# One order of instructions against another: half matmul groups, two token tiles' statistics on ScalarE, row maxima on GpSimd

## The chip, the core and the metric

The kernel runs on one core of a Trainium2 chip. The core has five engines that run their own instruction streams in order and meet only at semaphores: TensorE (PE, matmuls), VectorE (DVE), ScalarE (ACT), GpSimd (POOL) and SyncE (SP, here used only to issue DMAs). The metric is the device time of one execution in microseconds, the median of several runs. The kernel before takes 1212.65 us (three runs, 1212.34 to 1212.93).

## The reference

The input x is 2048 tokens by 512 features, in bf16. It is layer-normalised without scale or shift, and the result feeds two branches whose outputs are added to x:

```python
xn = _layernorm(x, axis=-1)
return x + _A_ref(xn, A_wqkv, A_wo) + _B_ref(xn, B_w1, B_w3, B_w2)

# A: 32 heads of 16 channels, every token attends to every token
scores = einsum("bhqd,bhkd->bhqk", q, k) * (16 ** -0.5)
o = softmax(scores) @ v            # then @ wo
# B: 512 -> 1792 -> 512
h = silu(xn @ w1) * (xn @ w3)      # then @ w2
```

The attention has 32 x 2048 x 2048 scores. Each must be part of a row maximum, and each must go through an exponential; nothing else in the computation has that many elements.

## The kernel before, in words

Four heads are a group: their 16-channel keys and queries lie in the four 32-partition strips of `KT` and `QT`, so four small matmuls run beside each other in TensorE. There are 8 groups of heads and 4 chunks of 512 queries, so 32 pairs of a chunk and a group. A pair is cut into *units* of 256 queries, the first pair into 128, 128 and 256, and the last three pairs into units of 128 (`units`, line 286).

The scores of a unit are computed twice.

- **Pass 1** (`p1_cand`, line 853). 128 queries of two heads against 512 keys, two matmuls into two PSUM banks (line 878). There are two such pairs of banks, 0-1 and 2-3. VectorE reduces each pair by one instruction, 1024 elements per partition to two maxima (line 900), into `part`. There are 1024 of these steps. The kernel calls them by their number n.
- **Final maximum** (`final_max`, line 906). Once all reductions of a unit are done, one more VectorE reduction takes the maximum over the four key chunks and negates it (line 941). GpSimd splits it into two bf16 parts in `Z` (lines 917 and 919). A transposing DMA and two row DMAs (lines 938 and 934) put these into rows 16 and 17 of each strip of `QT`, where the keys have ones, so that the next matmul subtracts the maximum by itself. For the first two units and the last four (`FAST_AUG`) a TensorE tile and a ScalarE copy do it instead (`tile_QT2`, line 684).
- **Pass 2** (`p2_cand`, line 974). The scores again, transposed, 128 keys by the unit's queries, one bank of 512 columns at a time (line 1014), in banks 4 to 7. ScalarE applies the exponential to a bank (line 1027), 2048 times in all, into one of 34 slots of `PT` (16 of them hold x at the start).
- **PV** (`tile_PV`, line 1035). Probabilities times V, with a column of ones in V that gives the denominator. ScalarE copies the result out (line 1091). The denominators go through DMAs and GpSimd (lines 1112 to 1136) to the normalised output. For the last three units VectorE does it with a reciprocal (line 1081).

Beside this run the *side tiles*, which accumulate in one bank and are then copied out by ScalarE: the transposes of the normalised input (`tile_tr`), the projections of K, Q and V, the gated network (`ffn_pair`: tiles G and U, three ScalarE instructions, lines 735 to 741, and three on GpSimd, lines 720 to 724), and the output tiles (`tile_OUT`). The results of the gated network wait in a ring of `NHT` = 28 slots of `hT`. The last four output tiles are made in two parts: `tile_OUTA` holds x and the gated network, `tile_OUTB` (VectorE, line 831) adds the eight head groups once they are normalised. A side tile is a list of *groups*, each of four matmuls of 512 columns in the four column strips (`col_groups`, line 487).

The order of all instructions is computed on the host before the program is emitted. `_Prog` keeps a clock for each engine from the constants at its top (`_VIS`, `_c_act`, `_c_dve`, `_c_mm`), and a loop takes again and again the step that could start first. `pick_pe` chooses between pass 1, pass 2 and a side group. A side group is taken if it ends before the moment when VectorE or ScalarE would run out of work (`late`). If none is ready and too little was issued lately (`low_load`), a *fill* is taken: four matmuls of the identity into a free bank, whose result nobody reads (`fill_cand`). What is decided by these clocks is then a fixed order. At run time each engine follows it and waits where it must.

The start: four DMAs bring x, four token tiles each (line 428). VectorE takes statistics of 16 token tiles (lines 502 and 505), GpSimd turns them into a factor (lines 515 to 523), VectorE normalises 12 tiles (line 530) and ScalarE four (line 535). Transposes, keys of group 0 and queries of group 0 follow, and then pass 1 can begin.

Of the kernel before, what the change touches and what calls it, by code (L numbers as in the profile page):

```python
# [13 lines left out]
_VIS = {"act": 0.155, "dve": 0.143, "pool": 0.085}  # L14
# [6 lines left out]
class _Item:  # L21
    __slots__ = ("fn", "reads", "writes", "occ", "lat", "cb", "pred", "name")

    def __init__(self, fn, reads, writes, occ, lat=None, cb=None, pred=None, name=""):
        self.fn = fn
        self.reads = reads
        self.writes = writes
        self.occ = occ
        self.lat = lat
        self.cb = cb  # L30
        self.pred = pred
        self.name = name


class _Prog:
# [3 lines left out]
    def __init__(self):  # L39
# [8 lines left out]
        self.pe_vis = 0.0  # L48

# [54 lines left out]
    def op(self, eng, fn, reads=(), writes=(), occ=0.1, lat=None, name="", first=None):  # L104
# [9 lines left out]
        op.vis = start + (occ + _VIS.get(eng, 0.1) if lat is None else lat)  # L114
        return self._add(op, reads, writes)

    def pe_start(self, mode, groups, ready):
        t = max(self.free["pe"], ready)
        if mode == "col":
            t = max(t, max(self.rg) + (0.09 if self.pe_mode == "row" else 0.0))  # L120
        else:
            t = max(t, max(self.rg[g] for g in groups))
            if self.pe_mode == "col":
                t = max(t, max(self.rg) + 0.104)
        return t

    def pe(self, fn, reads, writes, mode, groups, dur, name="", first=None):
# [8 lines left out]
        start = self.pe_start(mode, groups, ready)  # L136
        for g in (range(4) if mode == "col" else groups):
# [6 lines left out]
        if mode == "row":  # L144
            op.vis = max(self.pe_vis + 0.043, start + dur + 0.203)
# [60 lines left out]
class _Tile:  # L206
    __slots__ = ("groups", "evac", "name", "bank", "pred", "need", "on_start", "paced")

    def __init__(self, name, groups, evac, pred=None, need=None, on_start=None, paced=False):
        self.name = name  # L210
        self.paced = paced
        self.groups = groups
# [7 lines left out]
def _c_act(n):  # L220
    return n / 1200.0 + 0.063


def _c_dve(n):
    return n / 960.0 + 0.066


def _c_mm(n):
    return n / 2400.0 + 0.003
# [6 lines left out]
def _build(nc, A_x, A_wqkv, A_wo, B_w1, B_w3, B_w2, out):  # L236
# [16 lines left out]
    PV_LEFT = 4  # L253
    ROW_LEAD = 0.55
# [4 lines left out]
    NHT = 28  # L259
    UNIT_HEAD = (128, 128, 256)  # L260
    UNIT_TAIL = {1: (128, 128, 128, 128), 2: (128, 128, 128, 128), 3: (128, 128, 128, 128)}
    NFAST = 4
    NFPV = 3
# [12 lines left out]
    LOAD_WIN = 2.3  # L276
    LOAD_MIN = 14500
# [10 lines left out]
    NU = len(units)  # L288
    FAST_AUG = {0, 1} | set(range(NU - NFAST, NU))
# [8 lines left out]
    with ctx:  # L298
# [18 lines left out]
        wq_last = sb("wq_last", [128, DC * 4, 32], BF16)  # L317
# [15 lines left out]
        part = sb("part", [128, 2, 2, 4, NQC], FP32)  # L333
        negm = sb("negm", [128, 2, 8], FP32)
# [19 lines left out]
        OP_KEYS = [[("t1",)], [("a32",)], [("th", 0), ("th", 1)], [("zg", 0), ("zg", 1)]]  # L354

# [35 lines left out]
        poolq = {k: [] for k in ("z", "ln", "nrm", "ffn", "pad")}  # L391
# [1129 lines left out]
```

## Time and profile before

| what | value |
|---|---|
| median of three runs | 1212.65 us |
| profiled execution, first to last instruction | 1210.1 us |
| VectorE busy | 1191.3 us, 98% |
| ScalarE busy | 1160.9 us, 96% |
| TensorE busy (ends modelled) | 1158.3 us, 96% |
| GpSimd busy | 360.9 us, 30% |
| first pass-1 reduction starts | 18.47 us |
| last final maximum starts | 1190.91 us |

The profile page and the answers of the trace give the profiled execution. No time of its own is listed for it beside its span, so the 2.55 us between the span and the median stand for what lies around the instructions. Times are in microseconds from the first instruction unless ns is written. A busy time is the union of the records of an engine. Records of successive instructions on one engine overlap a little: a pass-1 reduction has a record of 1.21 us, but the next starts 1.13 us after it. So rates are read from starts, not from the mean of one record.

### The profile page before, as it was taken

To read this page: it belongs to the slowest core of one execution; us is meant where nothing else is said; L and a number is where in the kernel's file an instruction comes from. 1 tells how busy PE (TensorE), PEld (TensorE's weight loads), DVE (VectorE), ACT (ScalarE), POOL (GpSimd) and SP (SyncE) were. 2 spreads that over 40 slices of the span, in tenths; PEclk is the share of its full clock that TensorE was granted. 3 is DMA by queue.
4 is the path that set the end of the run, shared out by engine and by line. 5 is a ranking of instruction groups with operands and counts; after the bars stand their busy time and mean duration, and the time that the engine had idled before them with its cause. 6 is when DMAs were issued, how large, how long until landed. Compare 5 with 4: busy or idle time off the path is not lost.

```text
span 1210.1 us, 40652 instructions
## 1 busy us (share of the span) xinstructions
PE 1158.3 (96%) x17633; PEld 460.6 (38%) x17633; DVE 1191.3 (98%) x1154; ACT 1160.9 (96%) x2382; POOL 360.9 (30%) x470
## 2 busy tenths in 40 slices
PE   5999999999999999999999999999999999999998
PEld 2433333333333333333333333333333333334554
DVE  8999999999999999999999999999999999999995
ACT  5789999999999999999999999999999999999997
POOL 2234443635421135453111115553111111112210
PEclk9999999999999999999999999999999999999999
DMA  5422323222101022211001112211000111000000
GB/s 165 124 59 64 79 54 89 53 61 55 40 24 29 27 59 47 51 42 29 22 20 29 31 37 59 57 37 25 22 16 19 37 28 30 21 25 19 17 13 23
DMA packets 130303, 52.61 MB, mean 43 GB/s; under 512 B 99396, under 2 KB 130124, under 8 KB 130124
## 3 DMA queue, kind: packets, MB, share of 16 engines
q1 hardware_dynamic: 130124, 50.01, 16.4%
q8 instruction: 138, 2.26, 0.8%
q14 instruction: 41, 0.34, 0.1%
HBM read 38.73 MB, written 6.74 MB: 38 GB/s over the span
## 4 chain that ended last, share of the span: by engine, by line
ACT 49%; PE 33%; DVE 13%; issue 2%; POOL 1%; DMA 1%; SPq 0%; POOLq 0%
ACT PT L1027 42%; PE ps L491 18%; DVE part L900 13%; PE ps L1014 9%; PE ps L878 5%; ACT th L735 2%; ACT zg L737 2%; ACT U L1091 1%; ACT ub L741 1%; ACT kq L642 1%; PE ps L599 1%; ACT xnT L564 1%; DMA wk_on<-in_A_wqkv_dram 0%; POOL Rc L1116 0%; POOL hT L724 0%
## 5 line engine op out<-in xcount | busy, mean ns | idle before, releaser
L900 DVE TENSOR_REDUCE part<-ps 128x2 f32<-128x1024 f32 x1024 | 1167.8, 1214 | 1.8 <-PE ps L878 0.7
L1027 ACT ACTIVATE PT<-ps 128x512 bf16<-128x512 f32 x2048 | 1045.7, 650 | 6.1 <-PE ps L1014 5.0
L1014 PE MATMUL ps<-QT,KT 32*128 32x256 bf16 (+1 forms) x4544 | 566.9, 262 | 4.2 <-DVE wk_on L1083 0.3
L878 PE MATMUL ps<-KT,QT 32*128 32x512 bf16 x2048 | 437.6, 383 | 2.9 <-DVE part L900 2.3
L1014 PEld LDWEIGHTS ps<-QT,KT 32*128 32x128 bf16 x4544 | 215.7, 92 | 265.7 <-issue 108.0
L1116 POOL TENSOR_TENSOR Rc<-Lc,mone 128x8 f32<-128x8 f32 (+1 forms) x68 | 104.3, 1534 | 384.7 <-DMA Lc<-U 384.5
L491 PE MATMUL ps<-PT,Vaug 128*17 128x256 bf16 (+1 forms) x4544 | 191.0, 264 | 4.6 <-ACT zg L737 2.1
L491 PE MATMUL ps<-xnT,ident 128*32 128x512 bf16 x2048 | 162.0, 384 | 7.4 <-DVE part L900 0.5
L491 PE MATMUL ps<-xnT,w 128*32 128x512 bf16 x1792 | 149.0, 385 | 13.1 <-ACT zg L737 7.0
L878 PEld LDWEIGHTS ps<-KT,QT 32*128 32x128 bf16 x2048 | 113.6, 91 | 123.9 <-DVE part L900 56.4
L491 PEld LDWEIGHTS ps<-PT,Vaug 128*17 128x17 bf16 x4544 | 85.9, 89 | 100.6 <-issue 76.5
L722 POOL TENSOR_TENSOR a<-zg,ub 128x512 f32<-128x512 bf16 x56 | 64.6, 1153 | 61.8 <-ACT ub L741 61.6
L491 PE MATMUL ps<-w,hT 128*32 128x512 bf16 x896 | 79.7, 386 | 0.0
L724 POOL TENSOR_TENSOR hT<-a,t 128x512 bf16<-128x512 f32 x56 | 71.1, 1270 | 3.1
L491 PEld LDWEIGHTS ps<-xnT,w 128*32 128x32 bf16 x1792 | 39.3, 94 | 81.8 <-issue 72.1
L491 PEld LDWEIGHTS ps<-xnT,ident 128*32 128x32 bf16 x2048 | 40.1, 94 | 68.7 <-ACT PT L1027 50.1
L917 POOL TENSOR_SCALAR Z<-negm 128x8 bf16<-128x8 f32 (+1 forms) x70 | 15.7, 225 | 168.3 <-DVE negm L941 167.8
L1136 POOL TENSOR_TENSOR wk_on<-U,R 128x256 bf16<-128x256 f32 (+1 forms) x35 | 23.0, 658 | 105.2 <-DMA R<-rd 105.2
L1136 POOL TENSOR_TENSOR on_b<-U,R 128x256 bf16<-128x256 f32 (+1 forms) x33 | 23.4, 711 | 81.6 <-DMA R<-rd 81.5
L737 ACT ACTIVATE zg<-ps 128x512 bf16<-128x512 f32 x56 | 36.0, 643 | 0.0
L720 POOL TENSOR_SCALAR t<-th 128x512 f32<-128x512 bf16 x56 | 34.6, 618 | 4.6 <-ACT th L735 2.5
L741 ACT ACTIVATE ub<-ps 128x512 bf16<-128x512 f32 x56 | 35.7, 637 | 0.0
(78 smaller groups left out, 377.6 us busy)
## 6 DMA issues: line engine op xcount, KB each, us to landing
w<-in_B_w_dram SPq DMA_DIRECT2D x112, 128.0 KB
R<-rd SPq DMA_DIRECT2D x57, 128.0 KB
QT<-qd SPq DMA_DIRECT2D x31, 128.0 KB
KT<-kd SPq DMA_DIRECT2D x28, 128.0 KB
PT<-in_A_x_dram SPq DMA_DIRECT2D x4, 512.0 KB
xr<-in_A_x_dram SPq DMA_DIRECT2D x16, 128.0 KB
out_dram<-osb SPq DMA_DIRECT2D x16, 128.0 KB
qd<-kq SPq DMA_DIRECT2D x15, 128.0 KB
```

The lines of the kernel that those rows point to most:

```text
L491: ins = e.matmul(bank(bk)[32 * i:32 * i + m, c0:c0 + ncols], make_lhsT(i), rhs_ap(i), start=start, stop=stop, tile_position=(0, 32 * i), **kw)
L720: q.append(_Item(lambda e: e.tensor_scalar(t1[:, :], th[:, ss, :], 1.0, 1.0, ALU.mult, ALU.add), [("th", ss)], [("t1",)], 0.62, 0.72))
L722: q.append(_Item(lambda e: e.tensor_tensor(a32[:, :], zg[:, ss, :], ub[:, ss, :], ALU.mult), [("zg", ss), ("ub", ss)], [("a32",)], 1.1, 1.25))
L724: q.append(_Item(lambda e: e.tensor_tensor(hT[:, hslot(idx), :], a32[:, :], t1[:, :], ALU.mult), [("a32",), ("t1",)], [("hT", hslot(idx))] ...
L737: _Item(lambda e: e.activation(zg[:, ss, :], bank(bk), ACTF.Identity, scale=0.5), [("ps", bk)], [("zg", ss)], _c_act(512), cb=part_done, n ...
L741: return [_Item(lambda e: e.activation(ub[:, ss, :], bank(bk), ACTF.Identity), [("ps", bk)], [("ub", ss)], _c_act(512), cb=part_done)]
L878: ins = e.matmul(bank(2 * sl + i), QT[32 * j:32 * j + 32, qs, q * 128:(q + 1) * 128], KT[32 * j:32 * j + 32, g, kc * 512:(kc + 1) * 512], ...
L900: redq.append(_Item(lambda e: e.tensor_reduce(part[:, par, qt, 2 * pair:2 * pair + 2, kc], ps[:, sl * 1024:(sl + 1) * 1024].rearrange("p ( ...
L1014: ins = e.matmul(bank(b)[:, i * nq:(i + 1) * nq], KT[32 * j:32 * j + 32, g, (k0 + i) * 128:(k0 + i + 1) * 128], QT[32 * j:32 * j + 32, qs, ...
L1027: expq.append(_Item(lambda e: e.activation(PT[:, sl, :], bank(b), ACTF.Exp, scale=SCALE), [("ps", b)], [("PT", sl)], _c_act(512), cb=cb))
L1116: poolq["nrm"].append(_Item(lambda e: e.tensor_tensor(Rc[:, pp, 0:nl], Lc[:, pp, 0:nl], mone[:, 0:nl], ALU.pow), [("Lc", pp), ("mone",)], ...
L1136: poolq["nrm"].append(_Item(lambda e: e.tensor_tensor(onorm[ob][:, g, q0:q0 + nq], U[:, us, 0:nq], R[:, pp, 0:nq], ALU.mult), [("U", us)] ...
```

## The change

- *Half groups.* `col_groups` can issue a 512-column group as two of 256 columns. `pick_pe` takes a half where a whole group would end too late, and a half where little was issued lately.
- *Constants of the order.* New costs for ScalarE, VectorE and TensorE, among them a cold TensorE for the first 8 us; new leads and thresholds; another rule for fills, by a level that drains at 5000 columns per us and a window of 2.9 us; fills of ones at the very start.
- *The start.* x comes as 2, 2, 4, 4 and 4 tiles; the first 64 columns of the weights of K and Q come as small tiles of their own (`wk0c`, `wq0c`), ahead of the rest. Statistics of token tiles 2 and 3 are taken by ScalarE, by two activations with an accumulated sum. Eight tiles are normalised by VectorE and eight by GpSimd. Pass 1 of the first three units may go in the order in which key chunks get ready. V tiles may start earlier.
- *Final maxima.* For all units outside `FAST_AUG` the maximum over four key chunks is computed by six GpSimd instructions. Those of the first two units and the last four stay on VectorE.
- *The end.* The last four pairs, not three, go in units of 128. `tile_OUTA` takes six of the eight head groups, `tile_OUTB` the other two. The augmentation tiles (now `AQ`) get a bank before other tiles.
- *Memory.* `NHT` is 24, not 28.
- *Without effect.* `SPLIT` is empty, `PAIR_DEPTH` is 1, `MATE` is 0 and `TILE_BANKS` is None, so split rows, joined exponentials and bank choices in the new code never happen.

```diff
-    PV_LEFT = 4
-    ROW_LEAD = 0.55
+    PV_LEFT = 6
+    ROW_LEAD = 0.45
+    PAIR_DEPTH = 1
-    NHT = 28
+    NHT = 24
+    NGA = 6
-    UNIT_TAIL = {1: (128, 128, 128, 128), 2: (128, 128, 128, 128), 3: (128, 128, 128, 128)}
+    UNIT_TAIL = {i: (128,) * 4 for i in range(1, 5)}
-    LOAD_WIN = 2.3
-    LOAD_MIN = 14500
+    LOAD_RATE = 5000.0
+    LOAD_CAP = 3000.0
+    LOAD_MIN = 3000.0
+    RECENT = 2.9
+    RECENT_MIN = 9400.0
+    SPLIT = {u: ((1, 3),) for u in range(NU, NU)}
...
+        load_x(0, 2)
+        load_x(2, 4)
+        load_x(4, 8)
+        load_w(wk0c[:, :, :], [("wk0c",)], 1, 64)
+        load_w(wq0c[:, :, :], [("wq0c",)], 0, 64)
+        load_x(8, 12)
+        load_x(12, 16)
+        load_w(wv, WV_KEYS, 2)
+        load_w(wk, [("wk",)], 1)
+        load_w(wq[:, :, :], [("wq",)], 0)
...
+            f = part(0, ncols, start, skip or ncols == 512)
+            if ncols == 512:
+                f.halves = part(0, 256, start, True), part(256, 512, False, True)
             return f
...
+        LN_GROUPS = ((0, 2), (2, 4), (4, 8), (8, 12), (12, 16))
+        NORM = "ddpdp"
+        STATS = "dadddd"
...
+            if on_act:
+                for t in tl:
+                    miscq.append(_Item(lambda e, t=t: e.activation(
+                        a32[:, :], x_sb[:, t, :], ACTF.Identity, scale=1.0 / D, accum_out=mv[:, t, 0:1]),
+                        [("PT", t)], [("a32",), ("mv", t)], 0.57, 0.7))
+                for t in tl:
+                    miscq.append(_Item(lambda e, t=t: e.activation(
+                        a32[:, :], x_sb[:, t, :], ACTF.Square, scale=-1.0, bias=mv[:, t, 0:1],
+                        accum_out=mv[:, t, 1:2]),
...
+                p4 = part[:, par, 0:nqt, :, :].rearrange("p a j k -> p (a j) k")
+                d2, m2 = mx[:, 0, 0:4 * nqt, :], mx[:, 1, 0:4 * nqt, :]
+                poolq["z"] += [
+                    _Item(lambda e: e.tensor_tensor(d2, p4[:, :, 0:2], p4[:, :, 2:4], ALU.subtract), keys, [M0], 0.27),
+                    _Item(lambda e: e.tensor_scalar(d2, d2, BIG, 0.0, ALU.min, ALU.max), [M0], [M0], 0.27),
+                    _Item(lambda e: e.tensor_tensor(m2, d2, p4[:, :, 2:4], ALU.add), keys + [M0], [M1], 0.27),
+                    _Item(lambda e: e.tensor_tensor(d2[:, :, 0], m2[:, :, 1], m2[:, :, 0], ALU.subtract),
+                          [M1], [M0], 0.27),
+                    _Item(lambda e: e.tensor_scalar(d2[:, :, 0], d2[:, :, 0], 0.0, -BIG, ALU.min, ALU.max),
+                          [M0], [M0], 0.27),
+                    _Item(lambda e: e.tensor_tensor(ng, d2[:, :, 0], m2[:, :, 1], ALU.subtract),
+                          [M0, M1], [("negm", par)], 0.27)]
+                z_items()
...
+            if u not in FAST_AUG:
+                pool_max()
+                return None
...
-            groups = [g_on(qc, ts, g, g == 0, g == NG - 1) for g in range(NG)]
+            groups = [g_on(qc, ts, g, g == NGA, g == NG - 1) for g in range(NGA, NG)]
...
             if c[0] + c[2] <= late + TOL:
                 return c[0], c[1]
+            if recent_cols(c[0]) < RECENT_MIN and c[0] <= end + URG_WAIT:
+                return c[0], c[3] if len(c) > 3 else c[1]
+            if len(c) > 3:
+                if c[0] + _c_mm(256) <= late + TOL:
+                    return c[0], c[3]
             return go(x)
```

532 lines of the change are left out of this document (411 added, 121 removed).

## The prediction

> **What bounds the kernel now.** I read the busy shares first, then the chain that ended last, then busy time by stages, and last the reductions one by one. The first two seem to disagree:
>
> ```profile
> span 1210.1 us, 40652 instructions
> PE 1158.3 (96%) x17633; PEld 460.6 (38%) x17633; DVE 1191.3 (98%) x1154; ACT 1160.9 (96%) x2382; POOL 360.9 (30%) x470
> ...
> ACT 49%; PE 33%; DVE 13%; issue 2%; POOL 1%; DMA 1%; SPq 0%; POOLq 0%
> ```
>
> VectorE is the busiest, but the chain runs mostly over ScalarE. The stages (start:end and length, then busy us and instructions of PE, PEld, DVE, ACT, POOL, granted clock, DMA) decide it:
>
> ```profile
> 400.00:450.00 50.00, 49.16 (x698) 18.62 (x694) 50.00 (x48) 46.79 (x97) 13.42 (x18) 1.00 0.16 41
> ...
> 850.00:900.00 50.00, 48.25 (x714) 17.69 (x709) 49.91 (x48) 49.91 (x104) 8.22 (x11) 1.00 0.08 21
> ...
> 950.00:1000.00 50.00, 49.81 (x676) 18.39 (x668) 50.00 (x48) 46.33 (x95) 8.39 (x12) 1.00 0.11 30
> ```
>
> VectorE is full in each. ScalarE is full in one and idles 3 to 4 us in the others, where it has caught up and waits for rows whose maxima aren't there. So VectorE sets the pace, with ScalarE close behind: in windows of 25 us from 75 to 1200 us ScalarE idles about 20 us. Now VectorE's own stream (start, length of the run, count):
>
> ```profile
> 132.29 0.17 DVE L941 TENSOR_REDUCE negm<-part 128x8 f32<-128x32 f32 x1
> 132.38 18.19 DVE L900 TENSOR_REDUCE part<-ps 128x2 f32<-128x1024 f32 x16
> 150.49 0.17 DVE L941 TENSOR_REDUCE negm<-part 128x8 f32<-128x32 f32 x1
> 150.58 18.32 DVE L900 TENSOR_REDUCE part<-ps 128x2 f32<-128x1024 f32 x16
> ```
>
> A reduction takes (150.49 - 132.38) / 16 = 1.132 us. A final maximum has a record of 0.17 us but holds the next start back by only 0.09 (132.29 to 132.38). The 57 intervals between final maxima of whole units, from 40.53 to 1082.08 us, are 18.19 us at the least, 18.56 at the most, and together 4.7 us above 57 x 18.19. The twelve of 128 queries behind them lose 0.3 more. This is all that VectorE loses by waiting in mid-kernel.
>
> The head and the end are what is left:
>
> ```profile
> 4.83 2.47 DVE L502 BATCH_NORM_STATS2 stats<-PT 128x6 f32<-128x512 bf16 x4 [2.52 <-DMA PT<-in_A_x_dram]
> ...
> 12.96 3.20 PE L491 MATMUL ps<-xnT,wk_on 128*32 128x512 bf16 x32 [0.79 <-ACT xnT L564]
> ...
> 18.47 2.32 DVE L900 TENSOR_REDUCE part<-ps 128x2 f32<-128x1024 f32 x2
> ...
> 1190.91 0.17 DVE L941 TENSOR_REDUCE negm<-part 128x4 f32<-128x16 f32 x1
> ...
> 1193.66 0.27 ACT L696 ACTIVATE QT<-ps 128x128 bf16<-128x128 f32 x1
> ...
> 1202.35 2.17 ACT L1027 ACTIVATE PT<-ps 128x512 bf16<-128x512 f32 x4 [0.18 <-PE ps L1014]
> ...
> 1206.36 0.29 DVE L1083 TENSOR_TENSOR wk_on<-ps,R 128x128 bf16<-128x128 f32 x1
> ```
>
> Pass 1 runs from 18.47 to 1190.91. Behind it are 19.2 us: the last unit's maxima reach `QT` at 1193.66, and then 19 exponentials end at 1204.52, PV, reciprocal and store follow.
>
> **The change, part by part.** Durations are of this profiled execution, whose span is 1210.1; the median is 2.55 us more, which I carry over. Counts of the changed kernel are of its instruction order, which is fixed before it runs.
>
> *Final maxima.* The order holds 6 of the 71 on VectorE. 57 x 0.09 + 8 x 0.08 = 5.8 us leave it. It has no cover: VectorE is full on both sides of each. What is late next is GpSimd: 6 x 67 instructions, by the nearest row (line 919, 0.233 us) 94 us on an engine that is idle for 849. Bounds: 5.8 at the most; 0 if the pace passes to another engine (rival). I take **-5.8**.
>
> *The head.* Statistics start when x lands, at 4.83. Behind it 512 KB of weights are used at 7.91 after another 512 KB of x, so 1 MB takes 3.1 us, and a quarter of it less brings the first landing 0.75 us forward. Up to the first reduction VectorE did 16 statistics at 0.60, 16 aggregates at 0.09 and 8 normalisations at 0.33. The new order has 14, 14 and 6 there: 1.2 + 0.2 + 0.7 = 2.1 us less. Together 2.8; I take 2.4, as the short first groups may wait for GpSimd's factor (1.0 us for four tiles). Can TensorE deliver by 16.1? Its eight groups for K and Q took 3.20 us for 32 matmuls, about twice the 0.217 us a group later; with tiles 0 to 3 normalised by about 10 us, scores stand at 13.5 even so. The four statistics on ScalarE (0.60 by the copy of 512, line 642, to 0.83 by the normalisation, line 535) are 2.4 to 3.3 us while ScalarE otherwise waits for its first transpose at 10.85. GpSimd's eight normalisations, at 0.62 (line 720) to 1.15 (line 722), are off VectorE, and the first 8 reductions, 9 us, need only tiles 0 to 3. From the first reduction to n = 16 (40.84) the kernel before lost 40.84 - 18.47 - 16 x 1.132 = 4.3 us: four normalisations 1.4, two final maxima 0.2, waits 2.7. Two normalisations leave (0.7). Waits may go wholly or stay: I take 1.4 of 2.7, since three units can now feed key chunk 0. Head: 2.4 + 0.7 + 1.4 = **-4.5**, bounds -1.5 and -6.
>
> *Half groups and the new constants.* They can only win waits. A pass-1 step now stands behind a whole group at the worst, 0.217 us, then behind a half, 0.11. Bounds: all waits gone, -5.0; every whole unit as slow as the slowest, 57 x 0.37 - 4.7 = +16. I stay near the first row, the mean unit: one third of the waits of 4.7 would be 1.6, less what more instructions cost (19,651 matmuls for 17,635, which fit where the 0.10 of TensorE's time that fills take is). **-1.0**. [...] The row first: a pass-1 step starts at 34.16 and the next column group at 34.48, 0.32 later, where groups of one kind follow each 0.217; a change between row and column strips costs 0.10. The order makes 2418 such changes before and 2450 after. [...]
>
> *The end.* When the last pass-1 step is issued, 25 exponentials are left before and 32 after; behind the last unit's copy into `QT` stand 19 before and 27 after. ScalarE is the last engine there. Before, the 19 took 10.9 us (1193.66 to 1204.52), 0.56 each, since 24 matmuls of the output tile went between every 12 score matmuls. After, at most 16 go between; 27 at 0.49 (4.91 us for ten in mid-kernel) with the copy are 13.5. **+2.7**, bounds 0 (backlog eaten earlier) and +4.5 (0.56 again). The path from the last exponential to the store stays.
>
> *At nothing.* 24 slots instead of 28 hold network tiles back; side tiles in the order shift from n = 833-896 (97 groups to 71) to n = 961-1024 (4 to 88), where fills (70 to 9.5 groups) make room. On SP the extra chains of 128-query units add two net; its queue has gaps.
>
> Sum: -5.8 - 4.5 - 1.0 + 2.7 = -8.6. Span 1201.5, time 1212.65 - 8.6 = **1204.0**.
>
> **The rivals.**
>
> *The clock falls (slower).* Fills follow another rule. Counting matmul time between reductions, TensorE's array is used 0.66 before and 0.67 after, but the least over three successive reductions falls from 0.48 to 0.42. [...] At half the clock 0.67 becomes 1.33, so every us there costs 0.33 us. It decides from 11 us of loss, 33 us of low clock; 48 us, one short stretch in each 75, give +16: 1220. For it: the lower minimum. Against: no stretch of the kernel before, down to 0.48, shows a loss. [...]
>
> *ScalarE already bounds.* Then the 5.8 and 1.0 are idle time won, and the head's 4.5 less 0.4 us of its own added work and less 2.7 remains: 1211.3. For it: 49% of the chain, ever fewer idle stretches. Against: 20 us of idle ScalarE while VectorE has 5.
>
> *The GpSimd chain is late.* Six steps at 0.23 are 1.4 us, and the order lets network steps of up to 1.27 in between. The maxima come later, and ScalarE, where it has caught up, starves. As a constant lag this is paid once, at the end of the last unit that uses it: 1.4 + 1.27 = 2.7, giving 1206.7. It would need a lag that grows to cost more.
>
> **How the numbers follow.** Forecast 0.74 (its own range 1198.5 to 1209.5), ScalarE bound 0.10, late chain 0.08, clock 0.08. A measurement of this kernel tells 0.2%, 2.4 us, from no change. Faster: 0.74 + 0.08 and 0.03 of ScalarE's = 0.85; same 0.06; slower 0.01 + 0.08 = 0.09. The range must reach ScalarE's case and need not reach the clock's: 1198.5 (head -6 and all waits gone) to 1212.
>
> **What would show it.** First reduction near 16 us; 16 reductions in 18.10 us with no gap between units; the last final maximum near 1179.6; 22 us behind it. Wrong, if reductions lose more than 10 us to waits on TensorE, if ScalarE's backlog at the end is longer than 32 exponentials, or if groups of 512 columns show 0.43 us in mid-kernel.

## The result, and the profile after

The changed kernel takes 1217.16 us (median of 20 runs, 1212.02 to 1226.67) where the kernel before takes 1212.93 (20 runs, 1212.09 to 1213.88). The ratio is 1.0041, with a 95% interval of 1.0029 to 1.0053: slower by 0.4%, where I had forecast 1204.0 and a range that ended at 1212. The spread matters as much as the median: 14.7 us, against 1.8 before. The profiled execution took 1216.46 us, with a span of 1214.7.

The page after, busy shares, the granted clock in 40 slices, and the chain that ended last:

```profile
span 1214.7 us, 45008 instructions
PE 1173.5 (97%) x19649; PEld 486.4 (40%) x19649; DVE 1182.6 (97%) x1081; ACT 1170.0 (96%) x2389; POOL 450.8 (37%) x893
...
PEclk8999999999999999999999998999999999999999
...
ACT 42%; PE 40%; DVE 10%; DMA 4%; issue 2%; POOL 1%; SPq 0%; ACTq 0%
```

Before, the clock row read 9 in every slice:

```profile
PEclk9999999999999999999999999999999999999999
```

Two slices now read 8: the first, and the 25th, which begins at 729 us. TensorE's share of the chain rose from 33% to 40%. Stretches around that place show what happens there (start:end and length, then busy us and instructions of PE, PEld, DVE, ACT, POOL, granted clock, DMA):

```profile
720.40:723.80 3.40, 3.30 (x56) 1.38 (x58) 3.40 (x4) 3.40 (x9) 2.58 (x5) 1.00 0.57 148
723.80:727.20 3.40, 3.40 (x60) 1.20 (x48) 3.40 (x4) 3.40 (x9) 2.42 (x2) 1.00 0.43 100
727.20:730.70 3.50, 1.90 (x36) 0.78 (x36) 2.60 (x3) 1.76 (x5) 0.00 (x0) 0.99 0.18 40
730.70:740.90 10.20, 10.20 (x112) 3.27 (x104) 6.13 (x5) 6.68 (x13) 4.16 (x11) 0.50 0.10 21
740.90:744.30 3.40, 3.40 (x63) 1.20 (x56) 2.71 (x3) 2.83 (x7) 2.78 (x3) 1.00 0.37 80
```

TensorE does little in the third stretch, the clock is at half for the next 10.2 us, TensorE is then busy without a pause, and VectorE, the engine that set the pace, works for 6.13 of 10.20 us. The clock was at half from 89.0 to 92.4 us too, and in the head from 10.4 to 17.3 us.

Where the time went can be added up from VectorE's starts. Take 1.131 us for each step between reductions; what goes beyond it is lost. The fourth column is a version of the changed kernel that comes later.

| us | before | after | `t_lead_late` |
|---|---|---|---|
| first reduction starts | 18.47 | 19.09 | 19.45 |
| lost between reductions, first 64 | 3.51 | 4.78 | 3.33 |
| lost between reductions, the other 960 | 10.66 | 9.82 | 1.64 |
| from the last reduction's end to the end | 19.19 | 22.82 | 23.52 |
| span | 1210.1 | 1214.7 | 1206.2 |

The figures are of one profiled execution each. Of the changed kernel's 9.82 us, 6.25 lie in the 64 reductions around 730 us and 0.9 at 1137 us, where TensorE stood for 1.12 us; of the 4.78 in the first 64, 1.5 lie at 89 us. Most other blocks of 64 lose 0.02 to 0.11 us, where they lost 0.4 to 1.1 before. So the gain that I forecast for the reductions is there, and it is given back in a few places, where TensorE stands or its clock falls (2.2 of the 6.25 us go with the stand at 728 us, just ahead of the fall).

### The profile page after: what moved, and what is told of

Same layout as the page of the kernel before. It is cut to its first block, busy times and chain, and to the rows that moved or that the text cites. A ratio compares the mean times of both kernels' runs of the same rounds, so it can differ in the third digit from the quotient of the medians.

```text
span 1214.7 us, 45008 instructions
## 1 busy us (share of the span) xinstructions
PE 1173.5 (97%) x19649; PEld 486.4 (40%) x19649; DVE 1182.6 (97%) x1081; ACT 1170.0 (96%) x2389; POOL 450.8 (37%) x893
## 4 chain that ended last, share of the span: by engine, by line
ACT 42%; PE 40%; DVE 10%; DMA 4%; issue 2%; POOL 1%; SPq 0%; ACTq 0%
ACT PT L1266 36%; PE ps L543 22%; PE ps L1253 11%; DVE part L1031 10%; PE ps L991 7%; ACT th L806 2%; ACT zg L808 2%; DMA Zs<-Z 1%; DMA R<-rd 1%; ACT ub L812 1%; ACT U L1361 1%; DMA rd<-Rc 1%; ACT kq L712 1%; DMA QT<-Zs 0%; DMA PT<-in_A_x_dram 0%
## 5 line engine op out<-in xcount | busy, mean ns | idle before, releaser
L1266 ACT ACTIVATE PT<-ps 128x512 bf16<-128x512 f32 x2048 | 1056.9, 656 | 16.5 <-PE ps L1253 15.4
L1253 PE MATMUL ps<-QT,KT 32*128 32x256 bf16 (+1 forms) x4672 | 554.7, 259 | 5.0 <-DMA QT<-Zs 3.4
L1253 PEld LDWEIGHTS ps<-QT,KT 32*128 32x128 bf16 x4672 | 209.3, 92 | 239.0 <-issue 96.7
L543 PE MATMUL ps<-xnT,ident 128*32 128x512 bf16 (+1 forms) x2436 | 185.0, 358 | 8.0
L543 PE MATMUL ps<-xnT,w 128*32 128x512 bf16 (+1 forms) x2340 | 158.2, 337 | 7.8 <-ACT zg L808 5.8
L543 PEld LDWEIGHTS ps<-xnT,w 128*32 128x32 bf16 x2340 | 49.0, 95 | 87.7 <-issue 51.5
L543 PEld LDWEIGHTS ps<-xnT,ident 128*32 128x32 bf16 x2436 | 48.0, 94 | 81.3 <-ACT PT L1266 64.4
L1138 POOL TENSOR_TENSOR mx<-part 128x16 f32<-128x16 f32 (+1 forms) x67 | 14.1, 210 | 176.6 <-DVE part L1031 176.5
L543 PE MATMUL ps<-w,hT 128*32 128x256 bf16 (+1 forms) x1188 | 74.7, 331 | 0.0
L791 POOL TENSOR_SCALAR t<-th 128x512 f32<-128x512 bf16 x56 | 34.7, 619 | 14.6 <-ACT th L806 13.0
```

The lines of the kernel that those rows point to most:

```text
L543: ins = e.matmul(bank(bk)[32 * i:32 * i + m, c0 + a:c0 + b], make_lhsT(i), rhs if (a, b) == (0, ncols) else rhs[:, a:b], start=start, stop ...
L791: q.append(_Item(lambda e: e.tensor_scalar(t1[:, :], th[:, ss, :], 1.0, 1.0, ALU.mult, ALU.add), [("th", ss)], [("t1",)], 0.62, 0.72))
L1253: ins = e.matmul(bank(b)[:, i * nq:(i + 1) * nq], KT[32 * j:32 * j + 32, g, (k0 + i) * 128:(k0 + i + 1) * 128], QT[32 * j:32 * j + 32, qs, ...
L1266: expq.append(_Item(lambda e: e.activation(PT[:, sl, :], bank(b), ACTF.Exp, scale=SCALE), [("ps", b)], [("PT", sl)], _c_act(512), cb=cb, e ...
```

## The experiments

My first theory (1) was that the six GpSimd steps of a final maximum come late, that a score group of pass 2 then keeps TensorE waiting, and that the stand brings the clock down. These are TensorE's waits that named the rows of `QT` in the changed kernel (there were none before), and the start of the wait at 728 us in its stream:

```profile
PE ps L1253 <- DMA QT<-Zs: 3.4, 3, 1.6
```

```profile
728.14 0.39 PE L991 MATMUL ps<-KT,QT 32*128 32x512 bf16 x2
730.13 0.40 PE L1253 MATMUL ps<-QT,KT 32*128 32x256 bf16 x4 [1.60 <-DMA QT<-Zs]
730.45 0.88 PE L543 MATMUL ps<-PT,Vaug 128*17 128x256 bf16 x16
```

The rival (2) was that the new rule for fills lets TensorE run thin. Four kernels were for these two.

**All final maxima back on VectorE.**

```diff
-            if u not in FAST_AUG:
-                pool_max()
-                return None
```

> One part undone: the final maxima of all units are on VectorE again, all else as in the changed kernel, and the order is computed anew. Theory 1 (the row maxima come late by the six GpSimd steps, TensorE stands at its next score matmul until the row DMA lands, the gate halves its clock, and VectorE loses about 6 us to each such fall): no gap of TensorE over 0.6 us between 30 and 1190 us, no stretch at half clock there, runs within 1.5 us of each other, about 1207 us (the profiled 1214.7 less 8 us of two falls, plus 71 x 0.09 less 6 on VectorE, plus 2 around). Theory 2 (the new rule for fills leaves TensorE so little work that the gate falls by itself): falls at half clock stay, without a gap before them, and the runs spread over more than 8 us around 1217.

Measured: 1216.46 us (9 runs, 1213.14 to 1220.16), ratio 1.0031 (1.0017 to 1.0045). The granted clock of its runs went from 0.992 to 0.997, and the slower ones are those with the lower clock. The profiled run has no fall in mid-kernel, and loses 8.9 us between the last 960 reductions, about 0.45 in each 64. Taking the maxima off GpSimd thus gives up the gain of the reductions, but, by the clock, doesn't keep the falls away from all runs.

**The GpSimd maxima alone, put into the kernel before.**

```diff
+            if u not in FAST_AUG:
+                pool_max()
+                return None
             return _Item(lambda e: e.tensor_reduce(
```

> One part alone: the kernel before with the six GpSimd steps for the final maxima of the same units, nothing else of the change. Theory 1: the late maxima alone bring gaps of TensorE and stretches at half clock, and the runs spread upwards, 1208 to 1220 us, slower than 1212.9 in the median. Theory 2: old fill rule, so no falls; VectorE is freed of 65 x 0.09 = 5.8 us and the time is about 1207 with a spread under 1.5 us.

Measured: 1216.35 us (10 runs, 1213.72 to 1223.57), ratio 1.0034 (1.0019 to 1.005). The first 960 reductions lose 7.5 us where they lost 13.2; then the clock is at half from 1176.6 to 1190.3 us, and the end takes 27.6 us. TensorE never waited for the rows of `QT`, and its longest gap between 30 us and the fall is 0.72 us. A late chain is not needed for a fall. Nor is the fall all that kept this kernel from a gain: its two runs at a clock of 0.999, the level of the kernel before, took 1213.72 and 1214.20 us. In the profile 40 exponentials begin behind the start of the last reduction, where 25 did before, so ScalarE's backlog may have taken what VectorE won; no trace of an undisturbed run shows it.

**The transposes entered as late.** The order reckons 2.3 us for a transposing DMA; from its issue to that of the row DMAs the trace shows 2.3 to 4.5 us, 2.9 on average.

```diff
-                    [("Z", par)], [("Zs", par)], cb=rows_dma, occ=1.25)
+                    [("Z", par)], [("Zs", par)], lat=4.3, cb=rows_dma, occ=1.25)
```

> The changed kernel with one number of the order's costs changed: the transposing DMA of the maxima is taken to land 4.3 us after its issue, not 2.3 (the traces show 2.3 to 4.5). Theory 1: TensorE is given other work until the rows have landed, so gaps over 0.6 us and the falls behind them vanish or are one at most; about 1208 us, spread under 3 us. Theory 2: no difference to the changed kernel, 1217 with a spread over 8 us.

Measured: 1209.52 us (10 runs, 1205.33 to 1213.48), ratio 0.9974 (0.9959 to 0.9989), faster than both. Across its runs the span follows the clock: 1203.6 at 0.998, 1211.8 at 0.991. A straight line gives 1051 us of span for each 1 of clock (correlation 0.98); that of the changed kernel's 20 runs gives 983 (0.88), which is 0.41 us for each us at half clock. So the falls carry the spread of both. The line reaches a span of 1204.9 us at full clock, but no run can be there: the low stretch in the head, 6.8 us, and the one from 1211.9 us to the end take about 0.004 of the clock by themselves. At 0.996 the line gives a span of 1208.8, and a time of about 1210.6 us. That is an estimate; the highest clock of the 20 runs is 0.995.

**More fills.**

```diff
-    RECENT_MIN = 9400.0
+    RECENT_MIN = 12500.0
```

> The changed kernel with more fills: the window of 2.9 us must hold 12500 columns, not 9400; by the order the least use of TensorE's array over three reductions rises from 0.42 to 0.50, the kernel before had 0.48. Theory 1: a gap is a wait in order, which no fill behind it can close, so gaps and falls stay, 1214 to 1222. Theory 2: no stretch at half clock from 30 us on, and about 1208 with a spread under 2 us.

Measured: 1229.41 us (4 runs, 1224.30 to 1234.94), ratio 1.0138 (1.0094 to 1.0183). In the profile TensorE stood for the rows of `QT` for 2.6 us, and for 1.7 us again, and both times the clock fell within a microsecond of the wait's end. That the added work made the order run into these waits is likely, and not shown. Theory 2 in this simple form is out: fills everywhere are no remedy.

Next, each of the suspects alone.

**No half groups.**

```diff
-            if ncols == 512:
-                f.halves = part(0, 256, start, True), part(256, 512, False, True)
```

> The changed kernel with every 512-column side group whole again; maxima on GpSimd, new clocks, new fill rule and statistics on ScalarE stay. Theory 1 (the gain is taken back by falls of TensorE's clock, which come from an order that gives QT's transposes 2.3 us where they take 2.3 to 4.5 and so leaves stretches with little for TensorE): the halves are no cause of it, granted clock again 0.988 to 0.993, 1214 to 1219 us. Theory 3 (the halves themselves cost ScalarE: the step from one exponential to the next is 0.499 us in the changed kernel and 0.493 in the kernel before, 1772 of them are 11 us): the step goes back to 0.493 and the time falls by 4 us or more, to 1213 or less, with the clock as it was.

Measured: 1219.62 us (5 runs, 1216.86 to 1220.86), ratio 1.0051 (1.003 to 1.0073), clock 0.986 to 0.990. The step between exponentials went from 0.4993 to 0.4949, over half of the way back to 0.4929, so the halves do cost ScalarE some 8 us of work; but the time did not follow, since the reductions set it and the clock fell twice in the profile. Theory 3 explains a cost that is hidden.

**The old rule for fills.**

```diff
-            return load_at(st) < LOAD_MIN
+            return sum(w for t, w in recent if t >= st - 2.3) < 14500
...
-            if recent_cols(c[0]) < RECENT_MIN and c[0] <= end + URG_WAIT:
-                return c[0], c[3] if len(c) > 3 else c[1]
```

> The changed kernel with the kernel before's rule for filling groups (a fill when under 14500 columns were issued in 2.3 us) in place of the two new ones. Theory 1 with the late transposes as the cause: no change, clock 0.988 to 0.993, 1214 to 1219 us. Rival, the new rule lets TensorE run thin and that is what brings the falls: clock 0.996 or more after the head, 1206 to 1210 us.

Measured: 1217.82 us (10 runs, 1209.08 to 1228.73), ratio 1.0039 (1.0014 to 1.0064), clock 0.971 to 0.993, three falls in the profile. The old rule with the new order is no better.

**The late transposes in the kernel before.** The same edit as above, in the old kernel.

> The kernel before with the transposing DMA of a unit entered in the order as 4.3 us in place of 2.3, nothing else. It had no fall of the clock to lose. If the late transposes matter only where the order is tight (theory 1): 1211.5 to 1213.5 us, clock 0.999 to 1.000. If the entry is a gain of its own, whatever the order: 1208 to 1210.5 us, by the 3 us (and more) that it gave the changed kernel.

Measured: 1217.36 us (10 runs, 1215.40 to 1222.62), ratio 1.004 (1.0026 to 1.0053), clock 0.991 to 0.998. Neither expectation held. One number in the old order, with no instruction added (its trace has 60 matmuls fewer), cost 4.9 us and brought a fall at 1177.5 us, without any wait for the rows of `QT`. Not all of the 4.9 us need be the clock's, for the best run, at 0.998, still took 1215.40. Theory 1 fell with this run: what brings the falls is neither GpSimd nor late transposes, but something that most other orders have and the order before hardly has. Even that one isn't quite free of it: in the same session one of its 26 runs took 1217.32 us at a clock of 0.996, the others at most 1213.45 at 0.999 or more.

**The head, with late loads and more warm fills.**

```diff
-    DMA_RATE = 360.0
+    DMA_RATE = 200.0
-    WARM_FILL = 8.5
+    WARM_FILL = 12.5
```

> The changed kernel with the transposing DMA at 4.3 us, and the loads of x and the weights entered at 200 KB per us in place of 360, with warm fills until 12.5 us in place of 8.5. In the changed kernel's head the clock fell to 0.5 at 10.4 us and 32 K and Q matmuls took 3.60 us, and the first reduction began at 19.09 (19.26 with late transposes). If the cold clock holds the head: K and Q in 1.8 us, the first reduction near 17.4, and 1.8 us less than with late transposes alone (1209.5): near 1207.7. If the head is held by the loads, or ScalarE sets the end whenever VectorE starts: the first reduction at 18.5 or later, or an earlier one with the end where it was, 1209 to 1210.

Measured: 1218.93 us (10 runs, 1212.88 to 1223.62), first reduction at 19.98, and a wait of 4.8 us before the third. The edit made the head worse, and its order had a fall of 17.1 us at 1070 us. It settles nothing about the head.

**What stands before a fall.** All changes of the clock in a profile lie on one grid of 3.413 us, and low stretches are multiples of it (3.41 us at 89 us, 10.24 at 730 us). I cut each profile on its own grid and added up, for each window, the matmuls' columns times their share of the 128 rows, over 2400 columns per us, a round scale near the 512 / 0.217 = 2359 at which groups of 512 columns follow each other. I call it the rows at work. In the kernel before, the four matmuls of such a group start within 0.01 us of each other in their four column strips (19.05 to 19.06 us) and the next group 0.217 us later, so four strips of 128 rows come to 4 x 512 / 0.217 / 2400 = 3.93, and the "of a full array" in my expectations is loosely put. Two windows of the changed kernel by form, the one before the fall at 730.7 and an earlier one:

```profile
L543 PE MATMUL ps<-PT,Vaug 128*17 128x256 bf16 x20 | 1.1, 285 | 0.0
L1253 PE MATMUL ps<-QT,KT 32*128 32x256 bf16 x7 | 1.1, 270 | 1.6 <-DMA QT<-Zs 1.6
L991 PE MATMUL ps<-KT,QT 32*128 32x512 bf16 x4 | 0.8, 384 | 0.0
```

```profile
L991 PE MATMUL ps<-KT,QT 32*128 32x512 bf16 x6 | 1.4, 379 | 0.0
L1253 PE MATMUL ps<-QT,KT 32*128 32x256 bf16 x10 | 1.4, 273 | 0.0
L543 PE MATMUL ps<-xnT,w 128*32 128x512 bf16 x16 | 1.2, 384 | 0.0
L543 PE MATMUL ps<-xnT,wq 128*32 128x512 bf16 x12 | 0.8, 383 | 0.1
L543 PE MATMUL ps<-xnT,wq 128*32 128x256 bf16 x8 | 0.4, 278 | 0.0
```

The first is (20 x 256 + 7 x 256 / 4 + 4 x 512 / 4) / 2400 / 3.41 = 0.74, the second 2.17. Score matmuls use 32 of the 128 rows and take TensorE's time all the same: 384 and 379 ns a record in these two windows, where projections with all rows have 383 and 384. Over the 17 profiles of this study there are 17 falls between 25 and 1190 us, and 5724 windows that began at full clock, with 1.67 on average. Sixteen falls came right behind a window of 0.96 or less, the last behind one of 1.02. Of 64 windows below 0.97, 16 were followed by a fall. So a thin window seems needed, and isn't enough. TensorE's busy share doesn't tell these windows apart: it was up to 1.00 in the window before a fall. A plain count of columns over 2400 per us, without the weight of the rows, does so nearly as well: it was at most 1.58 before each fall and 2.23 on average, with 82 other windows as low, where by rows 64 others are. So that rows, and not columns, are what counts is not shown.

That gave theory 4: a fall needs a thin window; an order has some number of thin places; the grid lies differently in each run (steps of the clock's record begin at 15.62 us in the profile before and at 7.04 in the one after, 2.51 grid steps apart), so how many of them it hits is chance. The number can be counted from the order, without a run: three successive reductions (3.4 us) with under 0.95 of rows at work. The order before has 2 such places, the changed one 20, the same with late transposes 9, the old order with GpSimd maxima 17, and the old order with late transposes 16. Three kernels tested it with nothing but fills changed.

**The changed order, with its thin places filled.** 73 filling groups go ahead of score groups, into the bank that these overwrite; every other instruction stays in its place.

```diff
+                def f(e):
+                    if n in THICK:
+                        more(e)
                     for i, (j, c_) in enumerate(cells):
```

> The changed kernel with its order as it is on every engine, and 73 more filling groups (four 512-column matmuls each) put right ahead of a score group for a reduction, into the bank that it is about to overwrite, at the places where the changed kernel's trace has the least rows of TensorE at work in any 3.41 us. Theory 4 (the clock falls where the rows at work in one of the clock's 3.41 us windows are under some 0.95 of a full array, which the changed order lets happen for 16.4 us of its window starts and the kernel before for 3.9; the reductions' gain is real and given back there): no fall between 20 us and 1195 us in the profile, or one at most, granted clock 0.994 or more, reductions of mid-kernel at 1.13 us throughout; 1207 to 1211 us, since the profiled span of 1214.7 loses the 8.6 us of its slow stretches at 89, 730 and 1137. Rival (the falls come from waits and chance and not from thin stretches, and more matmuls only load TensorE further, as the 12500-column threshold did): clock 0.990 as before, 1217 us or more.

**The same for the order with late transposes**, with 66 groups.

> The same for the changed kernel with late transposes: its own order, 66 more filling groups ahead of score groups at its own thin places. Theory 4: no fall after the head in most runs, clock 0.996 or more, 1204 to 1208 us, faster than either kernel (late transposes alone: 1209.5, with the clock at 0.994 in the middle of its runs and 1205.3 in the best). Rival: no change from 1209.5, or slower by the load.

Measured: 1227.08 us (4 runs, 1226.90 to 1227.74) and 1226.81 us (4 runs, 1226.49 to 1227.19). The clock was 0.995 or 0.996 in all eight runs, no profile has a fall between the head and the last 4 us, and the spread over four runs each is 0.8 and 0.7 us, where it was 14.7 over 20 runs and 8.2 over 10. This half of theory 4 held. The time did not: the reductions now lose 25.4 us in place of 14.6. The stream shows the price; a score group stands 0.34 us behind the start of the fill ahead of it:

```profile
741.13 0.40 PE L543 MATMUL ps<-xnT,ident 128*32 128x512 bf16 x4
741.47 0.39 PE L995 MATMUL ps<-KT,QT 32*128 32x512 bf16 x2
```

Against the 6 us or so that the changed kernel loses without its slow stretches, 73 groups cost 19 us, 0.27 each. Where TensorE has few rows at work it need not be idle, so a fill there delays the next reduction. The falls were cheaper than this cure.

**The order before, with smaller fills in one place.**

```diff
+                if 249 <= p1_n[0] < 337:
+                    fg = col_groups(bk, lambda i: ident[:, 32 * i:32 * i + 32], lambda i: xnT[:, 0, 0:64], 64)
```

> The kernel before with its order as it is, and the filling groups between reductions 249 and 337 (300 to 400 us) cut from four 512-column matmuls to four of 64 columns: some 30 groups, about 20 us more of window starts with under 0.95 of the rows at work. Nothing that the outputs need is left out. Theory 4: the clock falls between 300 and 400 us in most runs, and there alone; the clock goes from 0.999 to about 0.995 and the time from 1212.5 to 1215 or more, with a wider spread. Rival (the falls come with waits on late transposes or GpSimd, which this doesn't touch): 1212.5, clock 0.999; TensorE has less to do and nothing waits.

Measured: 1220.97 us (4 runs, 1219.77 to 1221.78), ratio 1.0067 (1.0052 to 1.0082), clock 0.986 or 0.987 in all runs. The stretches of this kernel, and the middle one in the kernel before:

```profile
300.00:340.00 40.00, 37.10 (x538) 14.98 (x531) 40.00 (x39) 40.00 (x84) 19.16 (x23) 0.99 0.18 43
340.00:374.00 34.00, 33.99 (x378) 10.23 (x376) 27.81 (x25) 27.86 (x55) 4.47 (x5) 0.51 0.05 12
374.00:400.00 26.00, 25.86 (x348) 9.95 (x346) 25.59 (x25) 25.83 (x53) 3.93 (x7) 1.00 0.09 26
```

```profile
340.00:374.00 34.00, 33.32 (x470) 12.33 (x466) 34.00 (x33) 34.00 (x71) 5.64 (x8) 1.00 0.07 18
```

TensorE was given less to do, and the kernel got 8.4 us slower: 34 us at half clock in exactly the cut place, 25 reductions there in place of 33. Here thin windows brought the fall: the window before it had 0.39 of rows at work. Of the 10.0 us by which this profiled run is longer than that of the kernel before, 8.0 are lost by the 64 reductions there; 2.1 more are lost by the first 64, where the edit does nothing.

**All statistics on VectorE**, for the head.

```diff
-        STATS = "dadddd"
+        STATS = "dddddd"
```

> The changed kernel with all statistics on VectorE, to look at the head: the first reduction began at 19.09 us in the changed kernel and 18.47 before, where I had put 16.1. If the ScalarE statistics hold the head up: the first reduction by 18.5. If it is the load of x's third group (landed at 7.40) and the cold clock of the K and Q groups (3.60 us in place of about 1.8): 19 us again, and the time somewhere between 1212 and 1220 by the falls of its own order.

Measured: 1221.51 us (2 runs), first reduction at 20.16, two falls. The first reduction comes 1.1 us later than in the changed kernel, so the statistics on ScalarE don't seem to hold the head up. How much they help can't be read from one profile each: in the eleven profiles that keep the changed kernel's head, the first reduction starts between 18.03 and 19.59 us, later where the clock came back later (15.6 to 18.2 us). Where it came back at 17.3, as here, the first reduction started at 18.80 to 19.09.

What stayed open was whether any order of the changed kernel keeps its gain. I varied constants of the order, counted thin places in each, and took three with few: 2, 2 and 6.

```diff
s_lead_42:    ROW_LEAD 0.45 -> 0.42
t_lead_late:  ROW_LEAD 0.45 -> 0.42, LOAD_MIN 3000 -> 2700, transposing DMA lat 2.3 -> 3.3
u_lead_load:  ROW_LEAD 0.45 -> 0.42, LOAD_MIN 3000 -> 2700
```

> The changed kernel with ROW_LEAD 0.42 in place of 0.45, an order in which 2 stretches of three reductions have under 0.95 of the rows at work (20 in the changed kernel), and in which the mean over the kernel is 1.75 in place of 1.67, by 96 more filling groups. Theory 4 alone: clock 0.995 or more in nearly all runs, spread under 3 us, 1206 to 1209 us. If filling groups cost 0.27 us wherever they stand, as the 73 of the thick kernel did: no falls, but 1217 or more.

> The changed kernel with ROW_LEAD 0.42, LOAD_MIN 2700 in place of 3000 and the transposing DMA entered at 3.3 us: 2 thin stretches of three reductions, the mean of rows at work 1.70, 10 more filling groups than in the changed kernel. Theory 4: clock 0.995 or more in nearly all runs, 1206 to 1209 us, the steadiest and fastest of those with the maxima on GpSimd. If the falls were a matter of any change of the order and not of the count: clock 0.985 to 0.993, 1213 to 1219 us.

> The changed kernel with ROW_LEAD 0.42 and LOAD_MIN 2700: 6 thin stretches, the mean 1.68, 10 filling groups fewer than in the changed kernel. By the count it stands between late transposes (9 stretches, 1209.5 us) and the other two: theory 4 gives 1207 to 1211 us with one fall in about half of the runs, clock 0.992 to 0.998. If the count tells nothing: anywhere from 1209 to 1220.

Measured, against 1212.55 us of the kernel before on the same chip: 1207.59 (5 runs, 1207.22 to 1211.30), ratio 0.9966 (0.9953 to 0.9978); 1207.06 (1204.95 to 1208.02), 0.9954 (0.9941 to 0.9966); 1206.79 (1205.81 to 1209.14), 0.9953 (0.994 to 0.9967). All three are faster than both kernels, with clocks of 0.994 to 0.999, as theory 4 had it. It was not right in all: the spread of the first is 4.1 us where under 3 was expected, and the third, which was to be the slowest at 1207 to 1211, is the fastest. All three also share a `ROW_LEAD` of 0.42, and no order with that value and many thin places was run; these three alone can't tell the two apart. The second, on its page and in VectorE's stream (start, length of the run, count):

```profile
span 1206.2 us, 44910 instructions
PE 1164.3 (97%) x19585; PEld 474.8 (39%) x19585; DVE 1181.5 (98%) x1081; ACT 1173.5 (97%) x2389; POOL 452.4 (38%) x893
...
PEclk9999999999999999999999999999999999999999
```

```profile
698.86 61.33 DVE L1031 TENSOR_REDUCE part<-ps 128x2 f32<-128x1024 f32 x54
```

54 reductions in one run without anything between them: the clock row is full, and only 1.64 us are lost in 960 steps. `s_lead_42` has 96 fills more than the changed kernel and is fast too, so a fill in a place that the order chose doesn't cost the 0.27 us that one ahead of a score group did.

| kernel | thin places in its order | falls in the profile, 25 to 1190 us | median us |
|---|---|---|---|
| before | 2 | 0 | 1212.9 |
| `s_lead_42`, `t_lead_late`, `u_lead_load` | 2, 2, 6 | 0, 0, 1 | 1207.6, 1207.1, 1206.8 |
| `e_late_transpose` | 9 | 1 | 1209.5 |
| `o_late_head`, `g_stats_vector`, `m_before_late` | 14, 14, 16 | 1, 2, 1 | 1218.9, 1221.5, 1217.4 |
| `d_before_pool_max` | 17 | 1 | 1216.4 |
| after | 20 | 2 | 1217.2 |
| `b_old_fill`, `c_no_halves` | 31, 32 | 3, 2 | 1217.8, 1219.6 |

The orders differ in more than their thin places, so the last column is no measure of what one place costs. `a_max_on_vector` (8 places, no fall, 1216.5) lacks the maxima's gain; `i_more_fill` has none in its order, and got its two thin windows at run time, from the stands.

## Why the prediction was wrong

*Final maxima, -5.8, and waits, -1.0: right for VectorE's reductions, and a little small.* With the clock up, 960 reductions lose 1.64 us in `t_lead_late` and 10.66 before, which is 9.0 us gained where I had 6.8. With the maxima back on VectorE, in `a_max_on_vector`, 7.3 of these are lost again. The waits went nearly wholly. In the old order the same six steps won 5.7 us in the first 960 reductions, but no time. The group at 34.48 us in the kernel before came 0.10 us later than a group of its own kind would have; at that size the 32 more changes between row and column strips in the changed order would be 3.2 us. The 1.64 us that `t_lead_late` loses in 960 reductions leave no room for that, so such delays, if they came, were covered.

*The head, -4.5: wrong.* The first reduction starts at 19.09, not 16.1, and it takes 21.06 us to the sixteenth step behind it, as before (20.93). The lines of the changed kernel, VectorE and then TensorE:

```profile
3.75 1.29 DVE L572 BATCH_NORM_STATS2 stats<-PT 128x6 f32<-128x512 bf16 x2 [0.91 <-DMA PT<-in_A_x_dram]
4.96 0.30 DVE L575 BATCH_NORM_AGGREGATE mv<-stats 128x2 f32<-128x6 f32 x2
7.40 0.69 DVE L572 BATCH_NORM_STATS2 stats<-PT 128x6 f32<-128x512 bf16 x1 [2.15 <-DMA PT<-in_A_x_dram]
8.01 0.72 DVE L601 TENSOR_SCALAR osb<-PT,mv,lnr 128x512 bf16<-128x512 bf16 x2
8.65 1.87 DVE L572 BATCH_NORM_STATS2 stats<-PT 128x6 f32<-128x512 bf16 x3
...
10.52 0.70 DVE L601 TENSOR_SCALAR osb<-PT,mv,lnr 128x512 bf16<-128x512 bf16 x2
...
17.73 0.41 DVE L601 TENSOR_SCALAR osb<-PT,mv,lnr 128x512 bf16<-128x512 bf16 x1 [1.21 <-PE ps L634]
18.53 0.41 DVE L601 TENSOR_SCALAR osb<-PT,mv,lnr 128x512 bf16<-128x512 bf16 x1 [0.39 <-PE ps L634]
...
19.09 1.19 DVE L1031 TENSOR_REDUCE part<-ps 128x2 f32<-128x1024 f32 x1
```

```profile
9.11 0.74 PE L543 MATMUL ps<-ones_t 128*32 128x128 bf16 x40
11.05 1.01 PE L634 MATMUL ps<-ident,osb 128*128 128x128 bf16 x8 [1.19 <-DVE osb L601]
12.81 3.60 PE L543 MATMUL ps<-xnT,wk_on 128*32 128x512 bf16 x32 [0.75 <-ACT xnT L641]
```

The first x does land 1.08 us earlier, and VectorE has the 2.1 us less to do. But in order it then waits 2.15 us for the third load before it may normalise the first two tiles, and takes three more tiles' statistics before the second two. So the four tiles are normalised at 11.22, where before they were at 11.11. Later it waits 1.21 and 0.39 us for TensorE's transposes to free a buffer, while the first scores, whose matmuls end at 18.17, wait for it. The warm fills end at 9.85, the clock falls at 10.4, and the 32 K and Q matmuls take 3.60 us, where they took 3.20. The failing step is "with tiles 0 to 3 normalised by about 10 us, scores stand at 13.5": I moved work off VectorE without asking what its next instruction in order waits for, and left next to no time for the transposes and their copies. In the kernel before, K and Q began 1.85 us behind the fourth normalisation, and the first reduction 7.36 us behind it, so even a normalisation by 10 us would have given 17.4, not 16.1; the earliest start in the profiles with this head is 18.03. The slow groups of K and Q I had in the sum, at the old 3.20 us, and left them there. In the kernel before they start 0.43 us apart up to 15.50 us, and from 18.83 us groups of 512 columns start 0.22 apart; what ends the slow stretch, the trace does not show.

The 16 steps behind the first reduction rest on a misreading. 40.84 us is the start of n = 17, not 16; n = 16 starts at 39.40. The kernel before thus lost 3.1 us there, not 4.3, and waited 1.5 us, not 2.7, so the 1.4 us that I took from these waits would have been nearly all of them. Why nothing of it was gained was not tried.

*The end, +2.7: right, a little small.* 22.8 us where 21.9 would follow, against 19.2; 23.5 in `t_lead_late`. 31 and 35 exponentials begin behind the start of the last reduction where 25 did.

*The clock, a rival at 0.08: the step that failed.* The sum had no term for it. I saw the least use of TensorE's array fall from 0.48 to 0.42 and set it aside, because "no stretch of the kernel before, down to 0.48, shows a loss". That excludes nothing below 0.48, and 0.42 was below. The price that I gave, 0.33 us for each us at half clock, was near the 0.41 that the 20 runs show; the chance was what was wrong. The half was an assumption there, for no stage of the kernel before is below 1.00; the profile after has 0.50 from 730.7 to 740.9 us. No run shows one short stretch in each 75 us, the 48 us of low clock that my 1220 stood on: the profile after has 3.41 + 10.24 us between 25 and 1190 us. What the runs showed in its place: the changed order has 20 thin places where the old one has 2, the clock falls behind some of them in most runs, and VectorE loses its steps there. I should have counted how many thin places an order has, and not only its minimum. Nor does TensorE have to be idle for a fall: in `e_late_transpose` TensorE is busy for 16.63 of the 17 us before one, with no gap of over 0.1 us (the same columns as above; the ends of matmuls are modelled):

```profile
840.00:857.00 17.00, 16.63 (x237) 5.88 (x234) 17.00 (x16) 17.00 (x37) 3.32 (x7) 1.00 0.06 15
857.00:868.00 11.00, 11.00 (x126) 3.21 (x122) 8.54 (x8) 8.57 (x17) 2.33 (x8) 0.53 0.08 20
```

*At nothing (24 slots of `hT`, the chains on SP): no wait on either came up in what was looked at;* the one wait that names `hT` in the changed kernel is GpSimd's, 0.6 us. The time around the span, which I carried over as 2.55 us, is 1.76 in the profiled execution after.

*The GpSimd chain late, 0.08.* There is something of it: three waits of 3.4 us in all on the rows of `QT`, one of which made the window thin that brought the fall at 730 us. `d_before_pool_max` and three of the four fast versions have no such wait with the same six steps.

*ScalarE bounds, 0.10.* Not at the forecast's 1211.3: three versions with all its work run at 1207. But it is close. Between 75 and 1170 us it idles for 19.1 us in the kernel before and for 3.3 in `t_lead_late`. Its step between exponentials grew, from 0.493 to 0.499 us, which I had not foreseen, and most of that came from the half groups.

Added up, the forecast's parts with their measured sizes in `t_lead_late` are +1.0 for the start, -9.2 for the reductions and +4.3 for the end, -3.9 on the profiled span of 1210.1; the medians differ by 5.5. The 8.6 us of the forecast were never there, for the head's part alone was 4.5. In three other orders of the same change the gain is 5 to 6 us; in the changed kernel's own, the line over its runs leaves 2 us or so without falls in mid-kernel. What turned a gain into a loss of 4 us is the clock.

## What to carry to other kernels

Where TensorE is close behind the bounding engine, count its rows at work over any 3.4 us before you accept a new order; a change of one number in the order's costs lost 5 us in 1212 here, in part by this, and a run-to-run spread that grows from 2 to 15 us is the first sign of it. Compare orders at several settings of a constant, for one bad order says little of the change in it. Less work on an engine, or one more fill, is not safe by its sign: a cut in unread matmuls made the kernel before 8.4 us slower, and fills ahead of score groups made the changed one 10 us slower.

## What the runs showed of the hardware

The clock of TensorE fell without TensorE being idle: windows with 0.39 to 1.02 rows at work by the measure above, against 1.67 on average, stood before all 17 falls, while TensorE's busy time hardly dropped in some of them (16.63 of the 17 us before the fall in `e_late_transpose`). Low stretches lasted 3.41 to 34.1 us in steps of 3.413. A low stretch seems to prolong itself: of 60 windows at half clock, the 44 that were followed by another had 0.36 to 1.33 rows at work, the 16 behind which the clock came back 0.95 to 1.50. What decides between the 16 thin windows that were followed by a fall and the 48 that were not stays open; windows at 246 and 256 us in the changed kernel had 0.69 and 0.70, without a fall.
